# Attention, then two MLPs on one core: later and wider-spaced preparation of the first weight, and two ordering edges on VectorE and ScalarE

## The chip, the cores and the metric

The kernel runs on one core of a Trainium2 chip. The metric is the device time of one execution in microseconds (us); lower is better. Five engines work side by side: PE (TensorE) multiplies, DVE (VectorE), ACT (ScalarE) and POOL (GpSimd) do elementwise work, and SP (SyncE) issues most of the DMAs.

## The reference

Causal attention with a bias that decays by a running sum, four batches of eight heads, 576 positions, 64 numbers per head; then two MLPs on the 2304 x 512 result, the first with the square of a ReLU between its two weights, the second with a leaky ReLU.

```python
scores = scale * np.matmul(q, k.transpose(0, 1, 3, 2))
bias = -(cum[:, :, :, None] - cum[:, :, None, :])          # cum: running sum of max(s, 0)
scores = np.where(causal, -1000000000.0, scores + np.minimum(bias, 0.0))
attn = np.exp(scores - max); attn = attn / (sum + 1e-09)
x = (attn @ v) as (2304, 512)
x = np.maximum(x @ w_in, 0) ** 2 @ w_out                   # first MLP, 512 -> 2048 -> 512
x = leaky(x @ w2_in) @ w2_out                              # second MLP
```

## The kernel before, in words

**Attention (`attention`, L673 to L875).** The 32 (batch, head) problems go in 16 pairs of heads. Each pair has seven steps (`STEPS`), and a step is called a slot: pair x has slots 7x to 7x + 6, 112 in all. In a slot DVE adds the mask to a block of scores and takes its row minimum of the negated scores (`maxima`, L490), ACT takes the exponentials (L514), PE turns the result over (`flip`, L529), ACT or DVE copies it back (L552, L550), PE multiplies by the values (`values`, L571) and computes the scores of the blocks to come (`scores`, L469 and L457). The first reduction of a pair is the L490 row of form 128x128 at the pair's start.

**The first MLP's first layer (`up1`, L635).** Its 2304 columns are cut into five blocks of up to 512; blocks 0, 1 and 2 are computed inside the attention. `fill` (L774) hands out the matmuls of a block as units of three instructions (L663), three times in a slot, from slot 35 (`START[0]`) on. A block has 16 weight chunks (`fc`) of four units each; when a chunk's four units are issued, `close` (L640) takes the ReLU out of the PSUM bank on ACT (L642), which frees one of two banks called h, and squares it. For block 0 the first eight units go to chunks 0 and 1 in turn, so chunk 2 needs the bank of chunk 0.

**The operand of a block (`up1_x`, L623).** Four pieces of the attention's result are read back and split in a high and a low part: ACT copies the high part (L619), DVE subtracts for the low part (L620).

**The first weight (`load_w`, L158).** It arrives as 64-bit words and is turned into single precision in 16 chunks. A chunk is a job of six steps, one per slot: its first step has SP read 512 KB into one of two buffers (L154, tile `wst`); two steps do nothing; the fourth runs two ACT instructions (L114, L115: the words step); the fifth DVE's L117 and L120 and POOL's addition L122, the last to read the buffer; the sixth casts the high part on ACT (L169, chunks 0 to 9) or DVE (L171, chunks 10 to 15) and subtracts the low part on POOL (L172). The slots are set by

```python
CV = 11
...
at_slot(CV + 5 * fc // 2 + (4 if fc > 7 else 0) + gap, step, job)
```

so chunks 0 to 15 begin in slots 11, 13, 16, 18, 21, 23, 26, 28, 35, 37, 40, 42, 45, 47, 50 and 52. Later weights follow in the same buffers from slot 57 (`convert`).

**What sets the order.** A scheduler orders each engine's instructions by a planned timeline. On PE the order is written out from slot 35 on (`in_order`). `after(i)` adds an edge for the order alone: an instruction traced inside comes behind `i` in the queue if both are on the same engine. The jobs of a slot are traced behind the previous slot's last reduction and last exponential (`anchors`, L866):

```python
with after(*anchors, raw["last"]):
    for f, args in later.pop(y, ()):
        f(*args)
```

After the attention come blocks 3 and 4 and the three remaining layers; the change doesn't touch them.

Of the kernel before, what the change touches and what calls it, by code (L numbers as in the profile page):

```python
# [13 lines left out]
ALU = mybir.AluOpType  # L14
# [4 lines left out]
def f32(ap):  # L19
    return ap.bitcast(F32)  # L20
# [3 lines left out]
def attention_then_two_mlps(  # L24
# [24 lines left out]
    nc = tc.nc  # L49
# [8 lines left out]
    NR1 = S - R  # L58
    W = 512
    LAG = 2  # L60
    CV = 11
    SB, HN = 768, 384
    ORDER = (1, 7, 6, 2, 5, 4, 3)
    CHAIN = {1: 0, 6: 0, 5: 0, 3: 0, 7: 1, 4: 1, 2: 2}
# [307 lines left out]
            self.pT, self.sc, self.po = {}, {}, {}  # L372

    pairs = [Pair(b, g, i) for b in range(B) for g in range(H // 4) for i in range(2)]
    raw = {"fetched": None}

    def load_qk(at, x, i=None, which=(0, 1)):

# [95 lines left out]
    def maxima(at, x, kind, e):  # L474

        p = pairs[x]  # L480
        if kind == 3 and x < PLAIN:
            t = f32(p.Y[:, 3 * e])
        elif kind == 4 and x >= PLAIN:
            t = at.tile([P, S], F32, tag="yt", name="t", bufs=2)
        else:
            t = at.tile([P, S], F32, tag="t", name="t", bufs=TB)
        m = at.tile([P, 16], F32, tag="m", name="m", bufs=TB + 1)

        def reduce(sc, msk, a, z, first, m):
            return nc.vector.tensor_tensor_reduce(t[:, a:z], sc, msk, -QK_SCALE, first, ALU.add, ALU.min, m).ins  # L490

        sc = p.sc[kind][e]
        if kind == 0:
            tiles = ((0, P, 0), (P, 3 * P, 1))
            for a, z, c in tiles:
                done = reduce(sc[:, a:z], mask[:, S - z + a:], a, z, 3.0e38, m[:, c:c + 1])
        elif kind == 4:
            tiles = ((0, S, 0),)
            reduce(sc[:, :S // 2], mask[:, :S // 2], 0, S // 2, 3.0e38, m[:, 1:2])
            done = reduce(p.sc[kind][1][:, :S // 2], mask4, S // 2, S, m[:, 1:2], m[:, 0:1])  # L500
        else:
            tiles = ((0, (kind + 1) * P, 0),)
            done = reduce(sc[:, :(kind + 1) * P], mask[:, S - (kind + 1) * P:], 0, (kind + 1) * P, 3.0e38, m[:, 0:1])
        if kind == 0 and e == 0:
            p.sums = at.tile([P, 16], F32, tag="sums", name="sums", bufs=4)
        T = {0: 0, 2: 2, 3: 3, 4: 4}[kind]
        p.t = t
        return t, m, tiles, p.sums, 2 * T + e, done
# [106 lines left out]
                hs = slice(64 * e, 64 * e + 64)  # L615
                nc.vector.tensor_tensor(p.xo[hs, m:], p.xo[hs, m:], p.rb[4][hs, 64 - 64 * e:P - 64 * e], ALU.mult)

    def split(out, x):
        a = nc.scalar.activation(out[0], x, AF.Copy)  # L619
        b = nc.vector.tensor_tensor(out[1], x, f32(out[0]), ALU.subtract)  # L620
        return a.ins, b.ins

    def up1_x(mp, j, c, bufs):  # L623

        n, w = BLOCKS[j]
        xf = mp.tile([P, w], F32, tag="xf", name="xh", bufs=XF)
        nc.sync.dma_start(xf, xscr[c, :, n:n + w])
        yield
        t = mp.tile([P, 2, w], F32R, tag="xs", name="xs", bufs=bufs)
        xs[j, c] = t  # L630
        split([t[:, z] for z in range(2)], xf)

    xs = {}

    def up1(mp, j, tick=None):  # L635

        n, w = BLOCKS[j]
        group = 2 * W // w

        def close(fc, h, gs):  # L640
            g = gs[:, fc % group]
            done = nc.scalar.activation(g, h[:, :w], AF.Relu)  # L642
            if tick is None:
                nc.scalar.activation(g, g, AF.Square)
            else:
                squared = nc.vector.tensor_tensor(g, g, g, ALU.mult)
            if (fc + 1) % group == 0:
                nc.scalar.dma_start(gscr[fc + 1 - group:fc + 1, :, n:n + w].rearrange("f p t -> p f t"), gs)
            if tick is not None:
                tick(done.ins, squared.ins)  # L650

        order = [(fc, c) for fc in range(FC) for c in range(KC)]
        if tick is None:
            order[:2 * KC] = [(fc, c + x) for x in (0, KC // 2) for fc in range(2) for c in range(KC // 2)]
        todo, hs = None, {}
        for fc, c in order:
            if c == 0:
                if fc % group == 0:
                    gs = mp.tile([P, 2 * W], F32, tag="gs", name="gs", bufs=GB1).rearrange("p (f t) -> p f t", f=group)
                hs[fc] = bank("h")  # L660
            h = hs[fc]
            for y, (a, z) in enumerate(PASSES):
                nc.tensor.matmul(h[:, :w], win[fc][:, a, c * P:(c + 1) * P], xs[j, c][:, z, :w],  # L663
                                 start=(c == 0 and y == 0), stop=(c == KC - 1 and y == 2))
            if todo is not None:
                close(*todo)
                todo = None
            if c == KC - 1:
                todo = (fc, h, gs)
            yield  # L670
        close(*todo)

    def attention(at, mg, mx):  # L673
# [5 lines left out]
        def at_slot(y, f, *args):  # L679
            later.setdefault(y, []).append((f, args))  # L680
# [52 lines left out]
        for j in range(B):  # L733
            for c in range(KC):
                job = up1_x(mx, j, c, XS)
# [24 lines left out]
        for fc in range(FC):  # L760
            job = load_w(fc, wpool, stage)
            for gap in range(6):
                at_slot(CV + 5 * fc // 2 + (4 if fc > 7 else 0) + gap, step, job)
        for ch in range(BEFORE):
            job = convert(*divmod(ch, FC), stage, nc.sync, 3)
            for gap in range(6):
                at_slot(end - 5 * BEFORE // 2 - 8 + 5 * ch // 2 + gap, step, job)
        units, block, done = None, -1, 0
# [43 lines left out]
        for y in range(end + 14):  # L812
            x, st = divmod(y, n)
            if y == START[0]:
                fixed_from = len(nc.cur_bb.bb.instructions)
            if y < end:
                args = maxima(at, x, *STEPS[st])
                live[y] = args[0]
                behind = [args[-1], exponentials(*args[:-1])]
            fill(y, 0)  # L820
            tiled = len(nc.cur_bb.bb.instructions)
            for early in (True, False):
                for px in (x - 1, x):
                    if early or not 0 <= px < len(pairs):
                        continue
                    k0 = y - n * px
                    for region in range(2):
                        if k0 == values_at(px, region):
                            pairs[px].po[region] = values(px, region)
                for z in (y - 3, y - LAG, y - 1):  # L830
                    zx, zs = divmod(z, n)
                    kind, e = STEPS[zs]
                    if early != (kind == 0 and zx < ALONE):
                        continue
                    lag = {2: 3, 3: 1}.get(kind, LAG) if zx >= ALONE else LAG
                    if 0 <= z < end and (e or kind == 4) and y - z == lag:
                        flip(at, zx, kind, [live.pop(i) for i in range(z - e, z + 1)])
            if y + 1 < end and STEPS[(y + 1) % n][1] == 0:
                last = len(KINDS) * x + KINDS.index(STEPS[st][0])
                while asked <= last + (2 if last + 2 < AHEAD else 1):  # L840
                    scores(asked // len(KINDS), KINDS[asked % len(KINDS)])
                    asked += 1
            in_order(tiled, (nc.tensor.engine,))
            divided = [i for i in nc.cur_bb.bb.instructions[tiled:] if i.engine == nc.tensor.engine][-1:]
            for px in (x - 1, x):
                if not 0 <= px < len(pairs):
                    continue
                k0 = y - n * px
                for region in range(2):
                    if k0 == values_at(px, region) + (region or px >= ALONE):  # L850
                        gather(at, px, region, pairs[px].po[region])
                portions = ((5, 8, 9, 0, 2), (8, 11, 12, 2, 5)) if px < ALONE else ((9, 12, 12, 0, 5),)
                for inverted, spread_at, scaled, a, b in portions:
                    if k0 == spread_at and spread_at == scaled:
                        spread(px, a, b)
                    if k0 == scaled:
                        scale(px, a, b)
                    if k0 == inverted:
                        inverse(at, px, a, b)
                    if k0 == spread_at < scaled:  # L860
                        spread(px, a, b)
                if k0 == 12:
                    store(px)
            with after(*divided):
                fill(y, 1)
            with after(*anchors, raw["last"]):  # L866
                for f, args in later.pop(y, ()):
                    f(*args)
            if y < end:
                anchors = behind  # L870
            fill(y, 2)
# [307 lines left out]
```

## Time and profile before

| what | value |
|---|---|
| time, median of 3 runs | 932.47 us (927.65 to 934.24) |
| time of the profiled execution | 930.07 us |
| its span in the profile | 928.3 us |
| PE busy | 896.2 us, 97% of the span |
| DVE, ACT, POOL busy | 696.6, 580.8, 181.3 us |
| mean granted clock of PE | 0.993 of full speed |

The span runs from the first to the last instruction; the execution's own time is 1.8 us longer. Busy time is a union of instructions' times; the idle time of an engine matters where the chain that ends last goes through it.

### The profile page before, as it was taken

To read this page: it belongs to the slowest core of one execution; us is meant where nothing else is said; L and a number is where in the kernel's file an instruction comes from. 1 tells how busy PE (TensorE), PEld (TensorE's weight loads), DVE (VectorE), ACT (ScalarE), POOL (GpSimd) and SP (SyncE) were. 2 spreads that over 40 slices of the span, in tenths; PEclk is the share of its full clock that TensorE was granted. 3 is DMA by queue.
4 is the path that set the end of the run, shared out by engine and by line. 5 is a ranking of instruction groups with operands and counts; after the bars stand their busy time and mean duration, and the time that the engine had idled before them with its cause. 6 is when DMAs were issued, how large, how long until landed. Compare 5 with 4: busy or idle time off the path is not lost.

```text
span 928.3 us, 16360 instructions
## 1 busy us (share of the span) xinstructions
PE 896.2 (97%) x5902; PEld 809.6 (87%) x5902; DVE 696.6 (75%) x1265; ACT 580.8 (63%) x1097; POOL 181.3 (20%) x290
## 2 busy tenths in 40 slices
PE   5879999999999999999999999999999999999997
PEld 3646777777777778989999999999999999999997
DVE  5887666877774277688897997787488697886964
ACT  4788878878885454365555555686587754444442
POOL 4357763343430000001112101001110000000000
PEclk9999999999999999999999999999999999999999
DMA  9766858878853477948649326668668575628303
GB/s 166 173 180 171 223 154 227 224 212 231 231 180 105 126 248 270 317 155 258 218 158 355 112 97 219 215 207 322 239 219 299 176 253 151 183 57 210 81 14 55
DMA packets 229569, 178.48 MB, mean 192 GB/s; under 512 B 139600, under 2 KB 206352, under 8 KB 229488
## 3 DMA queue, kind: packets, MB, share of 16 engines
q1 hardware_dynamic: 192568, 105.13, 41.6%
q10 hardware_dynamic: 27048, 38.16, 11.2%
q0 software_dynamic: 9872, 34.15, 10.6%
q8 instruction: 46, 0.75, 0.3%
q14 instruction: 35, 0.29, 0.1%
HBM read 111.25 MB, written 66.13 MB: 191 GB/s over the span
## 4 chain that ended last, share of the span: by engine, by line
PE 57%; issue 9%; DVE 7%; DMA 5%; POOL 1%; ACT 1%; ACTq 0%; POOLq 0%; DVEq 0%
PE q L881 34%; PE h L663 17%; DVE op L988 3%; PE tr L571 2%; PE S L469 2%; PE tr L529 1%; DMA gp<-gscr 1%; DMA gp<-zscr 1%; DVE gp L982 1%; DMA gp<-qscr 1%; PE S L457 1%; DMA zscr<-post 1%; POOL zscr L1050 1%; DVE wt L119 1%; DVE gp L984 1%
## 5 line engine op out<-in xcount | busy, mean ns | idle before, releaser
L881 PE MATMUL q<-op,w 128*128 128x384 f32 x3024 | 528.3, 335 | 4.1 <-DVE op L988 2.9
L881 PEld LDWEIGHTS q<-op,w 128*128 128x128 f32 x3024 | 523.7, 188 | 8.4 <-DVE op L988 5.6
L987 ACT ACTIVATE op<-gp 128x768 fp32r<-128x768 f32 x189 | 158.3, 846 | 152.7 <-PE q L881 128.6
L663 PE MATMUL h<-xs,w 128*128 128x512 f32 (+1 forms) x960 | 211.7, 375 | 2.0 <-ACT gs L642 2.0
L988 DVE TENSOR_TENSOR op<-gp,op 128x768 fp32r<-128x768 f32 x189 | 178.2, 954 | 40.9 <-ACT op L987 39.6
L663 PEld LDWEIGHTS h<-xs,w 128*128 128x128 f32 x960 | 163.7, 189 | 38.8 <-issue 5.7
L514 ACT ACTIVATE t<-t,m 128x256 f32<-128x256 f32 (+4 forms) x134 | 75.9, 567 | 34.3 <-DVE m L490 32.0
L490 DVE CUSTOM_DVE_ANT_0 t<-S,mask 128x128 f32<-128x128 f32 (+4 forms) x119 | 49.4, 459 | 42.5 <-PE S L469 28.6
L642 ACT ACTIVATE gs<-h 128x512 f32<-128x512 f32 (+1 forms) x80 | 43.6, 547 | 48.0 <-PE h L663 47.7
L185 POOL DMA_DIRECT2D wscr<-wt x48 | 26.5, 553 | 234.9 <-DVE wt L120 234.6
L954 DVE TENSOR_TENSOR post<-q,post 128x768 f32<-128x768 f32 (+1 forms) x55 | 51.6, 940 | 15.7 <-PE q L881 15.2
L469 PE MATMUL S<-Y 64*128 64x128 f32 (+3 forms) x324 | 42.5, 366 | 12.8 <-DVE Y L427 7.6
L934 ACT ACTIVATE post<-q 128x768 f32<-128x768 f32 (+1 forms) x56 | 43.8, 781 | 12.5 <-PE q L881 12.4
L571 PE MATMUL tr<-pT,v 128*64 128x320 f32 (+3 forms) x384 | 48.6, 399 | 2.0 <-ACT pT L552 2.0
L114 ACT ACTIVATE wt<-wst 128x512 f32<-128x512 f32 x64 | 42.3, 660 | 11.2 <-DMA wst<-in_moe_w_in_dram 6.6
L120 DVE SCALAR_TENSOR_TENSOR wt<-wst,wt 128x512 uint32<-128x512 uint32 x64 | 46.7, 731 | 1.1
L914 ACT ACTIVATE post<-post 128x768 f32<-128x768 f32 x36 | 30.4, 845 | 25.8 <-DVE post L954 25.7
L571 PEld LDWEIGHTS tr<-pT,v 128*64 128x64 f32 x384 | 25.7, 141 | 23.3 <-issue 6.6
L117 DVE TENSOR_SCALAR wt<-wt 128x512 uint32<-128x512 uint32 x64 | 30.9, 483 | 19.0 <-ACT wt L114 18.8
L115 ACT ACTIVATE wst<-wst 128x512 uint32<-128x512 uint32 x64 | 42.8, 669 | 2.9 <-DMA wst<-in_moe_w_out_dram 1.7
L198 DVE TENSOR_TENSOR w<-wq,w 128x512 fp32r<-128x512 f32 x49 | 33.3, 688 | 14.4 <-ACT w L197 14.3
L550 DVE COPY pT<-tr 128x512 f32<-128x512 f32 (+1 forms) x64 | 33.7, 549 | 11.4 <-PE tr L529 11.4
(119 smaller groups left out, 931.7 us busy)
## 6 DMA issues: line engine op xcount, KB each, us to landing
gscr<-gs ACTq DMA_DIRECT2D x36, 512.0 KB
gp<-gscr SPq DMA_DIRECT2D x48, 384.0 KB
qscr<-post ACTq DMA_DIRECT2D x48, 384.0 KB
gp<-qscr SPq DMA_DIRECT2D x48, 384.0 KB
wscr<-wt POOLq DMA_DIRECT2D x48, 256.0 KB, 4.0
wst<-in_moe_w_in_dram SPq DMA_DIRECT2D x19, 512.0 KB
wst<-in_moe_w_out_dram SPq DMA_DIRECT2D x16, 512.0 KB
wst<-in_moe_w_out_dram POOLq DMA_DIRECT2D x16, 512.0 KB, 5.0
```

The lines of the kernel that those rows point to most:

```text
L120: nc.vector.scalar_tensor_tensor(t, hw, 0xC0000000, t, ALU.bitwise_and, ALU.bitwise_or)
L469: nc.tensor.matmul(p.sc[kind][e][:, a:z], qs[hs, T * P:(T + 1) * P], ks[hs, :z - a], start=(n == 0 and y == 0), stop=(n == len(tiles) - 1 ...
L490: return nc.vector.tensor_tensor_reduce(t[:, a:z], sc, msk, -QK_SCALE, first, ALU.add, ALU.min, m).ins
L514: done = nc.scalar.activation(t[:, a:z], t[:, a:z], AF.Exp, bias=m[:, c:c + 1], scale=-1.0, accum_out=sums[:, s0:s0 + 1])
L571: p.anchor = nc.tensor.matmul(po[64 * e:64 * e + 64, a:n], p.vr[:, c, e], rhs[e], start=(y == 0), stop=(y == len(mm) - 1), skip_group_chec ...
L642: done = nc.scalar.activation(g, h[:, :w], AF.Relu)
L663: nc.tensor.matmul(h[:, :w], win[fc][:, a, c * P:(c + 1) * P], xs[j, c][:, z, :w], start=(c == 0 and y == 0), stop=(c == KC - 1 and y == 2))
L881: i = nc.tensor.matmul(*args, skip_group_check=True, **kw).ins
L934: done = nc.scalar.activation(t[:, xs], acc, AF.Copy)
L954: done = nc.vector.tensor_tensor(t[:, xs], acc, t[:, xs], ALU.add)
L987: a = nc.scalar.activation(t[:, 0], src, AF.Copy)
L988: c = nc.vector.tensor_tensor(t[:, 1], src, f32(t[:, 0]), ALU.subtract)
```

## The change

It has three parts. The 16 chunks of the first weight begin in other slots: 17, 20, 23, 26, 29 and 32 for chunks 0 to 5, and 34, 36, 39, 41, 43, 45, 48, 50, 52 and 54 for chunks 6 to 15. DVE's subtraction of the operand split (L620) is put behind the last reduction traced so far, for blocks 1 and later. And the jobs of a slot are put, on ACT, behind the ReLU of chunk 0 or 1 of block 0, from when that is traced until chunk 2's is.

```diff
-    CV = 11
...
-    raw = {"fetched": None}
+    raw = {"fetched": None, "reduced": None, "closed": None}
...
-    def split(out, x):
+    def split(out, x, behind=None):
         a = nc.scalar.activation(out[0], x, AF.Copy)
-        b = nc.vector.tensor_tensor(out[1], x, f32(out[0]), ALU.subtract)
+        with after(behind):
+            b = nc.vector.tensor_tensor(out[1], x, f32(out[0]), ALU.subtract)
...
-        split([t[:, z] for z in range(2)], xf)
+        split([t[:, z] for z in range(2)], xf, raw["reduced"] if j else None)
...
             done = nc.scalar.activation(g, h[:, :w], AF.Relu)
+            raw["closed"] = done.ins if j == 0 and fc < 2 else None
...
-                at_slot(CV + 5 * fc // 2 + (4 if fc > 7 else 0) + gap, step, job)
+                at_slot((17 + 3 * fc if fc < 6 else 21 + 9 * fc // 4) + gap, step, job)
...
                 args = maxima(at, x, *STEPS[st])
+                raw["reduced"] = args[-1]
...
-            with after(*anchors, raw["last"]):
+            with after(*anchors, raw["last"], raw["closed"]):
```

## Rows read from the trace of the kernel before

**Rows 1.** Page, busy time of each engine over the span.
```profile
PE 896.2 (97%) x5902; PEld 809.6 (87%) x5902; DVE 696.6 (75%) x1265; ACT 580.8 (63%) x1097; POOL 181.3 (20%) x290
```
**Rows 2.** Windows, one per pair (1 to 6): stretch, length, busy, clock, DMA.
```profile
core 0: us, PE busy (x) PEld busy (x) DVE busy (x) ACT busy (x) POOL busy (x), PEclk, DMA share, GB/s
22.35:34.51 12.16, 10.76 (x123) 7.72 (x121) 9.09 (x34) 8.95 (x28) 2.37 (x9) 1.00 0.62 169
34.51:49.22 14.71, 11.93 (x135) 8.05 (x132) 12.28 (x40) 11.40 (x33) 7.97 (x12) 1.00 0.92 186
49.22:63.05 13.83, 10.90 (x113) 7.67 (x113) 11.25 (x40) 11.98 (x34) 8.60 (x12) 1.00 0.53 163
63.05:76.83 13.78, 11.56 (x93) 7.39 (x95) 11.78 (x41) 11.43 (x31) 8.62 (x11) 0.75 0.92 189
76.83:97.60 20.77, 19.02 (x171) 14.48 (x166) 15.83 (x45) 18.58 (x47) 16.02 (x23) 1.00 0.72 197
97.60:118.38 20.78, 20.78 (x172) 16.12 (x171) 13.92 (x41) 17.35 (x43) 14.38 (x17) 1.00 0.77 194
```
**Rows 3.** Timeline of DVE around the first reductions of pairs 3 and 4.
```profile
49.12 0.19 DVE L588 RECIPROCAL sums<-sums 128x5 f32<-128x5 f32 x1 [1.80 <-ACT sums L587]
49.22 0.25 DVE L490 CUSTOM_DVE_ANT_0 t<-S,mask 128x128 f32<-128x128 f32 x1
...
62.44 0.69 DVE L620 TENSOR_TENSOR xs<-xh,xs 128x512 fp32r<-128x512 f32 x1 [2.51 <-ACT xs L619]
63.05 0.28 DVE L490 CUSTOM_DVE_ANT_0 t<-S,mask 128x128 f32<-128x128 f32 x1
```
**Rows 4.** Timeline of ACT ahead of these two reductions.
```profile
45.46 0.67 ACT L114 ACTIVATE wt<-wst 128x512 f32<-128x512 f32 x1 [1.66 <-DMA wst<-in_moe_w_in_dram]
...
59.47 0.63 ACT L169 ACTIVATE w<-wt 128x512 fp32r<-128x512 f32 x1 [1.59 <-POOL wt L122]
...
61.77 0.64 ACT L619 ACTIVATE xs<-xh 128x512 fp32r<-128x512 f32 x1
```
**Rows 5.** Timeline of PE: the same values' matmuls in pairs 3 and 4.
```profile
53.82 2.16 PE L571 MATMUL tr<-pT,v 128*64 128x320 f32 x16
...
68.39 4.11 PE L571 MATMUL tr<-pT,v 128*64 128x320 f32 x16
```
**Rows 6.** Windows just ahead of the clock's fall and while it was down.
```profile
59.00:65.69 6.69, 4.62 (x56) 3.26 (x52) 4.11 (x18) 5.60 (x16) 5.43 (x7) 1.00 0.75 196
65.69:72.51 6.82, 5.88 (x34) 3.36 (x34) 6.55 (x19) 5.87 (x17) 3.03 (x3) 0.50 0.99 170
```
**Rows 7.** Timeline of ACT and PE at the first ReLU of block 0.
```profile
89.91 0.67 ACT L115 ACTIVATE wst<-wst 128x512 uint32<-128x512 uint32 x1
...
90.47 0.62 ACT L169 ACTIVATE w<-wt 128x512 fp32r<-128x512 f32 x1
90.99 0.58 ACT L642 ACTIVATE gs<-h 128x512 f32<-128x512 f32 x1
...
91.62 3.72 PE L663 MATMUL h<-xs,w 128*128 128x512 f32 x15 [1.75 <-ACT gs L642]
```
**Rows 8.** ACT by line and form, 24 to 160 us: count, busy, mean ns, idle before.
```profile
L115 ACT ACTIVATE wst<-wst 128x512 uint32<-128x512 uint32 x18 | 12.0, 669 | 1.1 <-DMA wst<-in_moe_w_in_dram 1.1
L114 ACT ACTIVATE wt<-wst 128x512 f32<-128x512 f32 x18 | 11.9, 663 | 3.1 <-DMA wst<-in_moe_w_in_dram 3.1
...
L169 ACT ACTIVATE w<-wt 128x512 fp32r<-128x512 f32 x10 | 6.3, 625 | 2.4 <-POOL wt L122 2.4
```
**Rows 9.** Waits of SP's queue, 24 to 160 us: total, times, longest.
```profile
SPq L154 <- POOL wt L122: 15.5, 5, 6.0
```
**Rows 10.** Waits of PE, 97 to 300 us: total, times, longest.
```profile
PE S L469 <- DVE m L490: 1.0, 1, 1.0
PE S L457 <- DVE m L490: 0.4, 1, 0.4
```
**Rows 11.** POOL finishes the last chunk; PE's row that first uses it.
```profile
141.46 1.29 POOL L172 TENSOR_TENSOR w<-wt,w 128x512 fp32r<-128x512 f32 x1 [1.94 <-DVE w L171]
...
154.71 3.02 PE L663 MATMUL h<-xs,w 128*128 128x512 f32 x12
```

## The prediction

> **What bounds the kernel now.** I read the page's busy times first: PE is busy for 97% of the span [rows 1], so what can still be won is PE's idle time and whatever makes PE slow. Next I cut the attention into windows, one per pair, at each pair's first reduction [rows 2]. Two regimes show. From pair 6 on PE is busy in all of 20.78 us, and the list of PE's waits from 97 to 300 us holds only 1.0 and 0.4 us [rows 10]: there PE is the bound and other engines' work is hidden. Pairs 1 to 4 have no filler matmuls; no engine is full in them, and a pair takes as long as its chain of scores, reductions, exponentials and turns. Pair 1, in which only one words step of a weight chunk falls and no cast, takes 12.16 us. Pairs 2, 3 and 4, with two words steps each beside their casts, take 14.71, 13.83 and 13.78: 2.55, 1.67 and 1.62 more, 5.84 in sum. Since PE is full nearly everywhere behind them, a microsecond won here should arrive at the end.
>
> Then I looked for what ends the waits at the starts of pairs 3 and 4. DVE works its queue in order. At 49.12 a reciprocal has waited 1.80 us for ACT, with the first reduction of pair 3 right behind it; at 62.44 the subtraction of an operand split has waited 2.51 us for ACT, with that of pair 4 behind it [rows 3]. ACT was late because weight work stood at the head of its own queue: a words step 1.66 us for its DMA, a cast 1.59 us for POOL's addition [rows 4]. So the weight chunks cost pairs 2 to 4 less by their length than by what queues behind them.
>
> Two more losses show. PE's granted clock was 0.50 from 65.69 to 72.51, which is 1.2 GHz in place of 2.4; in the 6.69 us before, PE had been busy for 4.62 [rows 6]. Sixteen value matmuls took 4.11 us there, and 2.16 one pair earlier [rows 5], 1.95 more. And in pair 5 PE stands 1.75 us until ACT has taken the first ReLU of block 0 out of its bank [rows 7].
>
> **The change part by part.** The sum is made against the profiled execution, 930.07 us (span 928.3). That is 2.4 below the median of 932.47 and inside the runs' 927.65 to 934.24.
>
> *Chunks later, ahead of slot 35.* Counting due slots, the words steps of pairs 2, 3 and 4 (slots 14 to 34) fall from eight (14, 16, 19, 21, 24, 26, 29, 31) to five (20, 23, 26, 29, 32): from three to one in pair 2, three to two in pair 3, and two in pair 4 either way. In the trace the words run some slots late, two to a pair. Pair 2 then holds one words step at its very end and no cast, so it is much like pair 1: of its 2.55 I take 2.0 off. Its buffers are empty, so the words step that waited for its DMA isn't there. Pair 3 keeps two chunks and casts, now three slots apart; a buffer is asked for again six slots after its last chunk began, not five, so waits like those of SP for POOL's addition, 15.5 us in five cases [rows 9], should shrink, and with them ACT's at the head of its queue. I take 0.2 off pair 3 and 0.3 off pair 4, whose two splits for block 0 stay where they are and get no edge. Sum -2.5. Bounds: all of the excess, -5.84, and +1.3, which is what a chunk cost in pair 2 (2.55 over two words steps), if the two chunks of pair 3 bunch up worse than now. I stay near the count of chunks, since the pair with none of their casts is the nearest row.
>
> What is late next in these pairs is PE: pair 1 has 10.76 us of PE in 12.16, so less than pair 1's length isn't to be had without moving scores.
>
> *The clock.* I put it at nothing: it falls again somewhere in pairs 2 to 4, or the time that it gives back is lost in a pair's chain. Its price by the matmul row is 1.95 us [rows 5]. The Trainium skill, "TensorE: Matmul & The Clock Gate", section "Part 1: The HAM clock gate", says that the slow state comes back after PE has been idle and that sustained work releases it. By that rule fewer idle stretches in pairs 3 and 4 would leave the clock up, which is a rival below; the trace agrees so far as the fall came behind 2 us of idle PE in 6.69.
>
> *Chunks later, behind slot 35.* Three more chunks are worked on there, 3 x (0.663 + 0.669 + 0.625) = 5.9 us of ACT [rows 8]. By due slots pair 5 gets the words and casts of chunks 5, 6 and 7; in the trace, where the work lags, it now holds three words steps and four casts as well, so pair 5 changes little. Pair 6 has three words steps now and no cast on ACT, and gets four and two: 1.33 + 1.25 = 2.6 us more against an idle 20.78 - 17.35 = 3.4 [rows 2]. It fits, at 96% of ACT. PE waited for ACT once, 1.75 us, in pair 5 with ACT at 89%, and never in pair 6 at 83%; I take a quarter of that wait, +0.4. Bounds 0 and +5.9. DVE and POOL have more room (13.92 and 14.38 of 20.78). SP issues the same 16 reads; behind a read that waits for a buffer stand the loads of q, k and v for pairs ahead. From slot 34 a buffer is asked for after 4.5 slots of 2.97 us, 13.4 us, longer than the five slots of about 2 us ahead of it, so I cost that at nothing.
>
> *The last chunks.* Chunk 15 begins two slots later, 5.9 us. POOL finishes it at 142.75 now, and PE's row with it starts at 154.71 [rows 11]: 12 us to spare, so nothing; if that were used up, the excess over 12 us would be paid once.
>
> *ACT behind the ReLU.* In the last rows before the ReLU, an L115 and an L169 run from 89.91 to 90.99 [rows 7]. Both were traced in slot 40, behind the ReLU of chunk 0; with the edge they come after it, and PE's stall falls by 1.08. Other due work in slots 39 to 41 (the turn of q, casts) waits for the ReLU too: behind it stand exponentials, and DVE's and POOL's halves of those jobs. Bounds: -1.75, and +1.6 if ACT now stands idle for PE as it did for POOL's addition [rows 4]. I take -1.1.
>
> *The split behind the reduction.* For blocks 1 and later it can only shift DVE's order in a stretch where PE lost 1.4 us in all to DVE [rows 10]. What is behind the moved subtraction is the block's matmuls, due slots later. Bounds -1.4 and +1.8 (a wait like that at 49.12, [rows 3], in the wrong place); I take 0, as PE is full in nearly all of this.
>
> Sum: -2.5 - 1.1 + 0.4 + 0 + 0 = -3.2, so 926.9 us, 0.6% below the median shown. Its own range, from half of the two gains to both plus a microsecond of noise, is 923.5 to 930.
>
> **The rivals.**
>
> *A, all of the chain comes back.* The clock stays at 2.4 GHz, the waits of rows 3 vanish, and pairs 2 to 4 come close to pair 1: -5.0 of 5.84, and all of the 1.75 in pair 5. 930.07 - 6.75 = 923.3. For it: the two stalls of rows 3 alone are 4.3 us. Against: pairs 3 and 4 still hold four chunks and two splits.
>
> *B, nothing.* What the early pairs gain is asked back when the same chunks' work and the same PE work come in pairs 5 and 6, and the ReLU waits for something else: 930. For it: not one instruction is removed, and no engine but PE is full. The Trainium skill, "Perfetto Trace Analysis", section "Identifying the Most-Contended Engine", says that kernels generally improve by improving the most-contended engine; that is PE by rows 1, and by that rule alone this change would give nothing. Against: pairs 1 to 4 aren't bound by PE.
>
> *C, slower.* ACT overflows in pairs 5 and 6. Its idle time there is 2.19 + 3.43 = 5.6 us [rows 2], and 5.9 us of chunk work moves behind slot 35. If the lag of the early chunks goes on, all of it lands in these two pairs, every exponential, turn and ReLU comes late by it, and PE, whose order is fixed, waits it out; a clock fall of 1.95 comes on top: -2.5 + 5.9 + 1.95 = +5.4, 935.4. It decides once ACT has over 20.8 us to do in one of the two pairs.
>
> *D, the weights come late:* each lost microsecond beyond the 12 to spare; about 933 if chunks 14 and 15 lag by another five slots.
>
> **How the numbers follow.** Forecast 0.40, A 0.25, B 0.22, C 0.10, D 0.03. The range of 920.0 to 934.0 holds the forecast, B, D and nearly all of A, with the bound of -5.84 and the runs' own spread; C lies outside. A measurement here tells about 1% from no change, 9.3 us: under 923.1 or over 941.8. Only the lower half of A and a tail of the forecast get under (0.13); C in its worst form gets over (0.03); the rest, 0.84, is within 1%.
>
> **What would show it.** The windows per pair: pair 2 near 12.5 us, pairs 3 and 4 at 13 to 13.7, pair 5 at 19.5 to 20 and pair 6 still near 20.8 with PE full. DVE's wait for the reciprocal at the end of pair 2 gone. PE's wait for L642 at 0.7 or less. The clock: down in pairs 3 or 4 for the forecast, up throughout for A. Wrong would be: pair 2 still over 14, or new PE waits for ACT of 2 us and more in pairs 5 to 7.

## The result, and the profile after

The changed kernel takes 937.64 us (median of 16 runs, 934.65 to 947.32) against 932.38 for the kernel before (16 runs). The ratio is 1.0065, 95% interval 1.0047 to 1.0084: slower, by about 5 us. The forecast was 926.9 in a range of 920.0 to 934.0. The profiled execution took 936.66 us, its span is 934.9 against 928.3, so 6.6 us are to be found.

The windows of the profile after, one per pair from pair 2 to pair 7, cut at the first reductions as in [rows 2] (columns as there):

```profile
33.60:47.69 14.09, 10.84 (x116) 7.42 (x114) 10.21 (x37) 8.83 (x28) 1.95 (x7) 0.98 0.89 183
47.69:60.66 12.97, 12.74 (x128) 8.95 (x124) 12.67 (x39) 11.29 (x33) 7.59 (x12) 0.89 0.61 176
60.66:72.83 12.17, 10.60 (x112) 7.25 (x113) 11.38 (x37) 11.59 (x33) 8.02 (x11) 1.00 0.98 184
72.83:100.43 27.60, 22.92 (x166) 16.83 (x166) 15.90 (x47) 19.23 (x47) 17.36 (x23) 0.94 0.57 150
100.43:123.93 23.50, 20.27 (x164) 14.75 (x164) 14.48 (x42) 19.08 (x47) 13.88 (x16) 1.00 0.76 198
123.93:144.19 20.26, 20.26 (x170) 15.70 (x169) 15.07 (x42) 16.81 (x41) 13.75 (x18) 1.00 0.56 174
```

Set beside [rows 2], pairs 2 to 4 take 39.2 us in place of 42.3, a gain of 3.1. Pair 5 takes 27.6 in place of 20.8 and pair 6 23.5 in place of 20.8: 9.5 lost. Pair 7 gives 0.5 back, pairs 8 to 14 differ by 0.1 in sum. The rest of the 6.6 is outside: pair 2 begins 0.9 us earlier (the last section says why), the stretch from pair 15 to the end takes 1.5 us longer. In pair 5 no engine is full; ACT, the engine that I had feared for, is idle for 8.4 of 27.6 us. So it is a wait, and the timeline of ACT names it:

```profile
76.36 0.63 ACT L168 ACTIVATE w<-wt 128x512 fp32r<-128x512 f32 x1
82.63 0.65 ACT L114 ACTIVATE wst<-wst 128x512 uint32<-128x512 uint32 x1 [5.64 <-DMA wst<-in_moe_w_in_dram]
83.19 0.64 ACT L113 ACTIVATE wt<-wst 128x512 f32<-128x512 f32 x1
83.73 0.60 ACT L513 ACTIVATE t<-t,m 128x384 f32<-128x384 f32 x1
...
84.33 1.13 ACT L618 ACTIVATE xs<-xh 128x512 fp32r<-128x512 f32 x2
```

(Line numbers after the change are one lower up to the split and up to two higher behind it; L114 was L115, L618 was L619.) The words step of chunk 5 stands at the head of ACT's queue for 5.64 us until its read has landed. Behind it stand an exponential of the pair and the last two operand splits of block 0, L618. In the kernel before, the same two splits stand ahead of the words step, which waits 0.97 us for its read, and PE takes the twelve matmuls of these splits without a wait:

```profile
82.63 1.14 ACT L619 ACTIVATE xs<-xh 128x512 fp32r<-128x512 f32 x2
84.73 0.67 ACT L114 ACTIVATE wt<-wst 128x512 f32<-128x512 f32 x1 [0.97 <-DMA wst<-in_moe_w_in_dram]
```
```profile
85.46 3.03 PE L663 MATMUL h<-xs,w 128*128 128x512 f32 x12
```

PE's timeline after shows who paid:

```profile
80.65 0.40 PE L468 MATMUL S<-ag 64*128 64x512 f32 x2
85.00 4.66 PE L664 MATMUL h<-xs,w 128*128 128x512 f32 x12 [3.95 <-ACT xs L618]
...
91.77 3.71 PE L664 MATMUL h<-xs,w 128*128 128x512 f32 x15 [0.73 <-ACT gs L642]
...
113.43 0.98 PE L664 MATMUL h<-xs,w 128*128 128x512 f32 x3 [0.91 <-ACT gs L642]
...
119.92 0.98 PE L664 MATMUL h<-xs,w 128*128 128x512 f32 x3 [1.84 <-ACT gs L642]
```

PE stood 3.95 us for the splits. The clock then ran at half speed for 3.4 us of pair 5 (mean 0.94), so that the twelve matmuls behind the wait took 4.66 in place of 3.03. The wait for the first ReLU fell from 1.75 us [rows 7] to 0.73. In pair 6 two more waits for a ReLU stand, 0.91 and 1.84; ahead of the first of them ACT again waited for a read of the weight, and the ReLU was queued behind:

```profile
109.95 0.66 ACT L113 ACTIVATE wt<-wst 128x512 f32<-128x512 f32 x1 [3.28 <-DMA wst<-in_moe_w_in_dram]
...
112.79 0.59 ACT L642 ACTIVATE gs<-h 128x512 f32<-128x512 f32 x1
```

The second, 1.84, is another case: from 109.95 to 119.26, where its ReLU starts, ACT is busy without a gap, with the work that had piled up and two more words steps.

By the windows PE was idle for 7.9 us of pairs 5 and 6, against 1.8 before; the four waits shown are 7.4 of it. The 3.4 us at half speed cost half of their length, 1.7. The last 1.7 of the 9.5 us are not accounted for.

Why did the read of chunk 5 land so late? The timelines of POOL and SP after, and a row of SP's waits from 60 to 100 us (total, times, longest):

```profile
72.58 1.30 POOL L121 TENSOR_TENSOR wt<-wt,wst 128x512 uint32<-128x512 uint32 x1
...
75.01 1.31 POOL L121 TENSOR_TENSOR wt<-wt,wst 128x512 uint32<-128x512 uint32 x1
```
```profile
75.03 0.95 SPq L627 DMA_DIRECT2D xh<-xscr  x2
76.07 0.93 SPq L153 DMA_DIRECT2D wst<-in_moe_w_in_dram  x2
```
```profile
SPq L627 <- DMA xscr<-xo: 1.4, 2, 1.2
```

The buffers were freed at 73.9 and 76.3. The read of chunk 5 didn't go at 73.9: it stood in SP's queue behind the reads of the last two pieces of block 0 (L627), which wait for the attention's result to be stored. So the reads of chunks 5 and 6 went out together at 76.07, and the first was there at 82.6, 6.6 us later.

### The profile page after: what moved, and what is told of

It reads as the page before. It is cut to its first block, busy times and chain, and to the rows that moved or that the text cites. A ratio compares the mean times of both kernels' runs of the same rounds, so it can differ in the third digit from the quotient of the medians.

```text
span 934.9 us, 16356 instructions
## 1 busy us (share of the span) xinstructions
PE 897.9 (96%) x5902; PEld 810.2 (87%) x5902; DVE 699.8 (75%) x1265; ACT 579.5 (62%) x1097; POOL 178.4 (19%) x290
## 4 chain that ended last, share of the span: by engine, by line
PE 60%; issue 9%; DVE 6%; DMA 3%; ACT 2%; POOL 1%; ACTq 0%; POOLq 0%; DVEq 0%; SPq 0%
PE q L883 38%; PE h L664 16%; DVE op L990 2%; PE tr L570 2%; PE S L468 2%; PE tr L528 1%; DMA gp<-zscr 1%; PE S L456 1%; DMA zscr<-post 1%; POOL zscr L1052 1%; DMA wst<-in_moe_w_out_dram 0%; DVE gp L984 0%; DMA xh<-xscr 0%; ACT w L196 0%; PE tr L605 0%
## 5 line engine op out<-in xcount | busy, mean ns | idle before, releaser
L664 PE MATMUL h<-xs,w 128*128 128x512 f32 (+1 forms) x960 | 214.4, 377 | 8.3 <-ACT xs L618 4.5
L489 DVE CUSTOM_DVE_ANT_0 t<-S,mask 128x128 f32<-128x128 f32 (+4 forms) x119 | 49.6, 458 | 33.3 <-PE S L468 19.9
L956 DVE TENSOR_TENSOR post<-q,post 128x768 f32<-128x768 f32 (+1 forms) x55 | 51.6, 940 | 15.9 <-PE q L883 15.5
L113 ACT ACTIVATE wt<-wst 128x512 f32<-128x512 f32 x64 | 42.3, 661 | 17.5 <-DMA wst<-in_moe_w_in_dram 12.1
L936 ACT ACTIVATE post<-q 128x768 f32<-128x768 f32 (+1 forms) x56 | 43.7, 781 | 12.5 <-PE q L883 12.3
L119 DVE SCALAR_TENSOR_TENSOR wt<-wst,wt 128x512 uint32<-128x512 uint32 x64 | 49.5, 774 | 1.3
L114 ACT ACTIVATE wst<-wst 128x512 uint32<-128x512 uint32 x64 | 42.9, 670 | 9.5 <-DMA wst<-in_moe_w_in_dram 7.2
L570 PE MATMUL tr<-pT,v 128*64 128x320 f32 (+3 forms) x384 | 46.3, 385 | 2.0 <-ACT pT L551 2.0
L528 PEld LDWEIGHTS tr<-ident,t 64*128 64x128 f32 x720 | 28.8, 140 | 17.8 <-issue 7.6
```

Source lines behind the costliest of these rows:

```text
L119: nc.vector.scalar_tensor_tensor(t, hw, 0xC0000000, t, ALU.bitwise_and, ALU.bitwise_or)
L570: p.anchor = nc.tensor.matmul(po[64 * e:64 * e + 64, a:n], p.vr[:, c, e], rhs[e], start=(y == 0), stop=(y == len(mm) - 1), skip_group_chec ...
L936: done = nc.scalar.activation(t[:, xs], acc, AF.Copy)
L956: done = nc.vector.tensor_tensor(t[:, xs], acc, t[:, xs], ALU.add)
```

## The experiments

Theory 1: the slots make the loss, through a words step at the head of ACT's queue. Theory 2: one of the two edges does. The first four runs take the change apart.

**The new slots without the edges**

```diff
-        split([t[:, z] for z in range(2)], xf, raw["reduced"] if j else None)
+        split([t[:, z] for z in range(2)], xf)
...
-            raw["closed"] = done.ins if j == 0 and fc < 2 else None
```

> The new slots without the two edges. Theory 1 (the slots are the loss: in pair 5 a words step stands at the head of ACT's queue and waits 5.6 us for the read of chunk 5, with the operand splits and exponentials behind it): pair 5 is again about 27 us against 20.8, ACT again waits over 4 us for the weight's DMA between 70 and 90 us, and the time is 936 to 940, ratio 1.004 to 1.009. Theory 2 (the edge behind the ReLU or the split makes the loss): pair 5 is near 20.8 and the time 927 to 930.

Measured: 936.82 us, ratio 1.0050 (1.0028 to 1.0072). Pair 5 takes 26.9 us. ACT's and PE's timelines show the same picture without either edge:

```profile
84.09 0.65 ACT L114 ACTIVATE wst<-wst 128x512 uint32<-128x512 uint32 x1 [5.26 <-DMA wst<-in_moe_w_in_dram]
```
```profile
86.46 0.50 PE L663 MATMUL h<-xs,w 128*128 128x512 f32 x1 [3.57 <-ACT xs L618]
```

**Both edges, with the slots of before**

```diff
-at_slot((17 + 3 * fc if fc < 6 else 21 + 9 * fc // 4) + gap, step, job)
+at_slot(11 + 5 * fc // 2 + (4 if fc > 7 else 0) + gap, step, job)
```

> Both edges, with the slots of before. Theory 1: no wait of ACT for the weight's DMA beyond that of before, pair 5 at 19.5 to 20.8 us, time 929 to 932.5, ratio 0.997 to 1.000. Theory 2: the loss is here too, 936 to 940.

Measured: 929.84 us, ratio 0.9987 (0.9971 to 1.0004), pair 5 at 20.7 us. PE is busy in all of that pair, at a mean clock of 0.92.

**The edge behind the ReLU alone, slots of before** (the slots as in the run above, and)

```diff
-        split([t[:, z] for z in range(2)], xf, raw["reduced"] if j else None)
+        split([t[:, z] for z in range(2)], xf)
```

> Only the edge behind the ReLU, with the slots of before. Theory 1: PE's wait of 1.75 us for the first ReLU falls to about 0.7 and the time by about 1 us, 930 to 932.5. Theory 2 with this edge to blame: pair 5 grows by several us and the time is over 935.

Measured: 929.02 us, ratio 0.9979 (0.9957 to 1.0001). Pair 5 takes 20.1 us, at a clock of 1.00, and PE's row behind the first ReLU has no wait left, where 1.75 us stood in [rows 7]:

```profile
88.84 0.58 ACT L642 ACTIVATE gs<-h 128x512 f32<-128x512 f32 x1
```
```profile
89.47 3.70 PE L664 MATMUL h<-xs,w 128*128 128x512 f32 x15
```

The stall is gone; the time just fails to tell itself from no change.

**The edge on the split alone, slots of before** (the slots as there, and)

```diff
-            raw["closed"] = done.ins if j == 0 and fc < 2 else None
```

> Only the edge that puts DVE's part of the split behind the last reduction, with the slots of before. Theory 1: nothing before 140 us changes, as block 0 has no such edge; PE's waits between 150 and 300 us change by 1.4 us at most; 931 to 933. Theory 2 with this edge to blame: pairs 9 and 13, where the splits of blocks 1 and 2 fall, grow and the time is over 935.

Measured: 932.45 us, ratio 1.0004 (0.9980 to 1.0027): nothing. With these four Theory 2 is out: the slots are the loss. The next four ask what in the slots it is: a words step at the head of the queue (1a), or the amount of weight work moved behind slot 35 (1b).

**The changed kernel, words step of chunk 5 three slots later**

```diff
-        for _ in range(3):
+        for _ in range(6 if fc == 5 else 3):
             yield
...
-            for gap in range(6):
+            for gap in range(9 if fc == 5 else 6):
```

> The changed kernel, with the words step of chunk 5 alone due three slots later; its read keeps its slot. In the order of ACT the two instructions then stand behind the operand splits of block 0 and one exponential, no longer ahead of them. Theory 1a (the loss in pair 5 is what is queued on ACT behind the words step that waits for its read): PE's wait of 3.95 us for the splits is gone or under 1.5, pair 5 is 22 to 25 us in place of 27.6, the time 932 to 935.5. Theory 1b (what costs is the amount of weight work behind slot 35, not who stands at the head): pair 5 stays at 26 or more and the time at 936 to 939.

Measured: 932.68 us, ratio 0.9998 (0.9978 to 1.0017), so some 5 us under the changed kernel. But pair 5 is still 27.3 us; that half of the expectation missed, and the timelines of ACT, DVE and PE say why:

```profile
78.17 1.33 ACT L618 ACTIVATE xs<-xh 128x512 fp32r<-128x512 f32 x2 [0.54 <-DMA xh<-xscr]
82.56 0.66 ACT L114 ACTIVATE wst<-wst 128x512 uint32<-128x512 uint32 x1 [3.06 <-DMA wst<-in_moe_w_in_dram]
...
84.32 0.66 ACT L113 ACTIVATE wt<-wst 128x512 f32<-128x512 f32 x1 [0.51 <-DMA wst<-in_moe_w_in_dram]
```
```profile
85.01 0.43 DVE L116 TENSOR_SCALAR wt<-wt 128x512 uint32<-128x512 uint32 x1 [4.67 <-ACT wt L113]
...
88.17 0.68 DVE L489 CUSTOM_DVE_ANT_0 t<-S,mask 128x512 f32<-128x512 f32 x1
```
```profile
80.86 3.03 PE L664 MATMUL h<-xs,w 128*128 128x512 f32 x12
...
89.52 1.09 PE L456 MATMUL S<-Y,last 128*128 128x288 f32 x3 [5.29 <-DVE m L489]
```

The splits now run at 78.17, 6.2 us earlier than in the changed kernel, as soon as their input is there (its reads went out at 75.51 here and at 75.03 there). PE's 3.95 us for them are gone, and the same twelve matmuls take 3.03 us. But another wait comes to the front: DVE's half of a words step, queued ahead of the pair's next reductions, stands 4.67 us for ACT, and PE stands 5.29 for the reduction. The L113 that DVE waits for, at 84.32, waits for a read that landed after the one that the L114 at 82.56 waits for; by the order of the reads it is that of chunk 6, whose words step was not moved. In the changed kernel DVE had stood about as long, beside ACT's own stall:

```profile
83.86 0.43 DVE L116 TENSOR_SCALAR wt<-wt 128x512 uint32<-128x512 uint32 x1 [4.88 <-ACT wt L113]
```

With PE's 5.29 us the clock fell, and it stayed at half speed for 6.8 us, twice as long as in the changed kernel (the pair's mean is 0.88); fifteen matmuls took 5.47 us, 3.71 in the changed kernel at full speed:

```profile
91.60 5.47 PE L664 MATMUL h<-xs,w 128*128 128x512 f32 x15
```

Of the 4.2 us between the spans of the two profiles, 2.6 come in pairs 6 and 7 (41.2 us in sum against 43.8) and 1.4 from pair 15 on. So this run shows that the order on ACT decides what PE waits for; that pair 5 comes back with it, it doesn't show.

**No chunk from slot 30 to 35**

```diff
-at_slot((17 + 3 * fc if fc < 6 else 21 + 9 * fc // 4) + gap, step, job)
+at_slot((17 + 3 * fc if fc < 5 else 26 + 2 * fc) + gap, step, job)
```

> Both edges, chunks 0 to 4 in the new slots, chunk 5 from slot 36 and the rest every two slots to slot 56: no chunk begins between slots 29 and 36, as none does between 28 and 35 in the kernel before. Theory 1a: no wait of ACT for the weight's DMA ahead of the splits, pair 5 at 19.5 to 21.5; what pairs 0 to 4 won (about 4 us) arrives, 927 to 930, unless the closer reads make new waits in pairs 6 to 8. Theory 1b: even more weight work lies behind slot 35, so 937 to 942.

Measured: 930.25 us, ratio 0.9987 (0.9960 to 1.0015). Pair 5 takes 18.6 us, 9 under the changed kernel and 2.1 under the kernel before:

```profile
72.48:91.10 18.62, 18.62 (x157) 14.26 (x158) 14.73 (x44) 17.68 (x44) 14.88 (x21) 1.00 0.66 165
```

The 2.1 are not all won. A window ends at DVE's first reduction, and PE's work can fall into the next one: 157 matmuls stand in this one, 171 in that of the kernel before [rows 2]. Over pairs 5 to 7 it is 61.8 us, against 62.4 before and 71.4 in the changed kernel. Pairs 6 and 7 take 21.9 and 21.2, and a new loss stands in pair 8, 25.7 us against 20.8: PE is idle for 3.0 us of it, and the clock's mean is 0.93.

**The gap, with one chunk more ahead of it**

```diff
-at_slot((17 + 3 * fc if fc < 6 else 21 + 9 * fc // 4) + gap, step, job)
+at_slot((14 + 3 * fc if fc < 6 else 36 + 9 * (fc - 6) // 4) + gap, step, job)
```

> Both edges, chunks 0 to 5 every three slots from slot 14, chunk 6 from slot 36 and then every two and a quarter, to 56. Theory 1a: as the run before, one chunk fewer behind slot 36 and reads further apart, so pair 5 at 19.5 to 21 and 926.5 to 930; pairs 2 to 4 give back about 1 us. Theory 1b: 935 to 939.

Measured: 929.34 us, ratio 0.9973 (0.9953 to 0.9992). Pair 5 takes 18.7, pair 8 24.2. The timelines of SP, ACT and PE in pair 8:

```profile
139.20 5.06 SPq L388 DMA_DIRECT2D qr<-in_q_dram  x4
144.36 0.66 SPq L151 DMA_DIRECT2D wst<-in_moe_w_out_dram  x1
```
```profile
149.07 0.68 ACT L114 ACTIVATE wst<-wst 128x512 uint32<-128x512 uint32 x1 [5.18 <-DMA wst<-in_moe_w_out_dram]
```
```profile
151.18 0.32 PE L605 MATMUL tr<-ident,sums 128*128 128x128 f32 x1 [1.23 <-ACT xo L580]
```

The same kind of wait in another place: the first read of the next weight came behind the loads of k and q in SP's queue, and its words step stood at ACT's head for 5.18 us. PE is idle for only 1.2 us of the 24.2; the window holds 182 matmuls, 173 in the kernel before. Over pairs 5 to 8 this kernel takes 84.1 us, the kernel before 83.2.

**The kernel before without its pause of four slots**

```diff
-at_slot(CV + 5 * fc // 2 + (4 if fc > 7 else 0) + gap, step, job)
+at_slot(CV + 5 * fc // 2 + gap, step, job)
```

> The kernel before without its four slots of pause ahead of chunk 8 (chunks 8 to 15 begin in slots 31, 33, 36, 38, 41, 43, 46 and 48); no edges. Theory 1a: now a read and a words step fall where block 0's last two pieces are read and split, PE waits 2 to 5 us for the splits or the first ReLU in pair 5, 933 to 938. Theory 1b: less weight work behind slot 35 than before, so 929 to 932.

Measured: 937.34 us, ratio 1.0056 (1.0035 to 1.0077), with pairs 5 and 6 at 24.7 and 25.1 us. This kernel has less weight work behind slot 35 than the kernel before, and no edge; it loses as much as the change:

```profile
85.21 0.65 ACT L115 ACTIVATE wst<-wst 128x512 uint32<-128x512 uint32 x1 [3.39 <-DMA wst<-in_moe_w_in_dram]
...
86.91 1.14 ACT L619 ACTIVATE xs<-xh 128x512 fp32r<-128x512 f32 x2
```
```profile
87.58 0.49 PE L663 MATMUL h<-xs,w 128*128 128x512 f32 x1 [2.04 <-ACT xs L619]
```

Theory 1b is out: more work behind slot 35 with a pause gained, less without one lost. The last three runs try to keep the gain of pair 5 without the loss of pair 8.

**The early gap, then every two slots**

```diff
-at_slot((17 + 3 * fc if fc < 6 else 21 + 9 * fc // 4) + gap, step, job)
+at_slot((14 + 3 * fc if fc < 6 else 24 + 2 * fc) + gap, step, job)
```

> Both edges, chunks 0 to 5 from slot 14 every three as in the run with the early gap, the rest from slot 36 every two slots, so that the last begins in 54 and not in 56. In that run pair 5 had gained 2 us and pair 8 lost 3.4, where a words step of the next weight waited 5.2 us for a read that SP issued behind the loads of q and k. If it is the bunching of the last chunks with that weight that costs, pair 8 comes back to 21 and the time is 925 to 928; if the wait only depends on where the next weight's read stands among the loads, pair 8 stays at 24 and the time at 929 to 931.

Measured: 928.54 us, ratio 0.9977 (0.9963 to 0.9992). Pair 8 is back at 19.9 us, better than expected; the time lies between the two ranges, as pairs 6 and 7, where reads now follow each other closer, take 21.5 and 21.7, 2 us more in sum than with the wider spacing. Pairs 5 to 8 take 81.8 us.

**The same, and the later weights three slots later**

```diff
-at_slot(end - 5 * BEFORE // 2 - 8 + 5 * ch // 2 + gap, step, job)
+at_slot(end - 5 * BEFORE // 2 - 5 + 5 * ch // 2 + gap, step, job)
```

> As the run before, and all 19 chunks of the later weights three slots later (from slot 60). On the same theory of a wait at the head of ACT's queue, the words step no longer meets a read stuck behind q and k: pair 8 at 20.8 to 21, 924 to 928. Against it: at the end of the attention the later chunks run up to slot 110 and may hold up pair 15 or the blocks behind it by 1 to 2 us.

Measured: 928.57 us, ratio 0.9977 (0.9961 to 0.9994): no gain over the run before, where pair 8 had nothing more to give, and just over the 928 expected.

**The gap from 36, and the later weights three slots later** (the edit of the run with no chunk from slot 30 to 35, and the one above).

> The run whose chunks 5 and on begin from slot 36 every two slots, with the later weights three slots later. There pair 8 was 25.7 us. On the theory it comes down to 21 to 22 and the time to 925 to 928; if its loss came from chunk 15 itself (56) being late for the matmuls, it stays at 24 to 26 and 929 to 931.

Measured: 927.29 us, ratio 0.9954 (0.9935 to 0.9973), the fastest of the study, with pair 8 at 21.2 us in place of 25.7. In its profile the clock stays up through the whole attention. SP's, ACT's and PE's side of pair 5:

```profile
75.76 0.93 SPq L153 DMA_DIRECT2D wst<-in_moe_w_in_dram  x2
```
```profile
77.38 1.38 ACT L618 ACTIVATE xs<-xh 128x512 fp32r<-128x512 f32 x2 [0.25 <-DMA xh<-xscr]
...
83.25 0.67 ACT L113 ACTIVATE wt<-wst 128x512 f32<-128x512 f32 x1
```
```profile
72.40:91.00 18.60, 18.60 (x157) 14.26 (x158) 14.69 (x45) 17.68 (x44) 14.82 (x21) 1.00 0.66 164
```

The two reads go out at 75.76, as they did at 76.07 in the changed kernel. Here the words step comes at 83.25, with its data there and the splits, exponentials and the ReLU ahead of it, and PE is busy in all of the pair. That pair of profiles says it best: the read goes out as late in both and costs pair 5 nothing here; the words step placed ahead of the splits is what costs. No run moved the words steps of chunks 5 and 6 alone, with every other slot of the changed kernel kept.

## Why the prediction was wrong

The sign was wrong because of one term. Both signs of being wrong that I had named came up: pair 2 over 14 us (14.09), and a new PE wait for ACT of over 2 us (3.95). Point by point:

- **Chunks later, ahead of slot 35: right in sum by luck, not by pair.** I took 2.0, 0.2 and 0.3 us off pairs 2, 3 and 4, 2.5 in sum; they fell by 0.6, 0.9 and 1.6, 3.1 in sum. For pair 2 I had argued that with empty buffers no words step would wait for its DMA. The reads of chunks 0 and 1 were issued together, at 39.42, and ACT and PE show the wait, with the copies that PE needed behind it:

```profile
44.40 0.66 ACT L113 ACTIVATE wt<-wst 128x512 f32<-128x512 f32 x1 [2.91 <-DMA wst<-in_moe_w_in_dram]
```
```profile
46.00 0.58 PE L528 MATMUL tr<-ident,t 64*128 64x64 f32 x11 [1.84 <-ACT xo L580]
```

  Pair 4 gave 1.6 in its place. Its clock was 1.00 and no longer 0.75; how much of the 1.6 is the clock's no run separates (with both edges and the slots of before pair 4 took 13.4 us at 1.00, but with a PE wait of 1.6 us for POOL in it). And SP's waits for POOL's addition, which were to shrink from 15.5 us [rows 9], were 19.3 us from 24 to 160.
- **The clock: put at nothing.** It fell at the border of pairs 2 and 3, as the forecast had it, and in pair 3 that cost nothing: PE was busy for 12.74 of 12.97 us, and for 11.49 of 13.00 in the last run, where the clock didn't fall:

```profile
47.20:60.20 13.00, 11.49 (x126) 8.10 (x122) 12.68 (x40) 11.36 (x33) 7.53 (x13) 1.00 0.63 177
```

  It fell again in pair 5, behind the new wait, and there the fall cost 1.7 us.
- **Chunks later, behind slot 35: the step that failed.** I put +0.4, by comparing the sum of ACT's work with its idle time, and costed the reads at nothing since a buffer comes up again after 4.5 long slots. Pairs 5 and 6 lost 9.5 us, beyond my bound of 5.9 too. The sums were right: ACT was busy for 19.2 and 19.1 us there, within the 20.8 that I allowed. Wrong was to ask only for room. I had seen this very kind of wait in [rows 4] and counted it as a cost of the old slots; I didn't ask where the new slots would put it. The pause between slots 28 and 35 stood in the code that I described, and the new slots fill it just where the last two pieces of block 0 are read (slot 33) and split (slot 38). Taking the pause from the kernel before costs the same 5 us; with a pause in the new slots the 5 us are not there.
- **Rival C had the sign and the place, not the mechanism.** A late ReLU, PE waiting it out and a clock fall came as it said. But an overflow of ACT would have shown ACT full, and it was idle for 8.4 us of pair 5 and 4.4 of pair 6; only the 1.84 us of pair 6 came where ACT had no gap. The Trainium skill, "TensorE: Matmul & The Clock Gate", section "Architectural detail: the array is 16× 32×32, not 1× 128×128", says that ACT and DVE take their instructions strictly in order. The traces agree: the splits ran at 84.3 in the changed kernel, behind the words step, though in the run with that step later the same input, read 0.5 us later, was there at 78.2.
- **ACT behind the ReLU: right by the profile.** -1.1 predicted; alone it took the whole wait of 1.75 us away, 0.7 off pair 5 and 0.8 off pair 6. The ratio of 0.9979 (0.9957 to 1.0001) fits that and doesn't rule out nothing. In the changed kernel 0.73 was left, as a cast ahead of the ReLU waited for POOL.
- **The split behind the reduction: right,** at nothing (1.0004).
- **The last chunks: right,** no wait for them appeared behind pair 6.
- **The range beside the sum.** Its lower end, 923.5, doesn't follow from its words: both gains and a microsecond give about 925.5.

What stays open: the 1.5 us that the changed kernel's profile loses from pair 15 on. From 300 us on PE's waits there sum to 5.8 us, against 4.3 before: 1.2 more for ACT's L936, 0.6 new for a split, 0.3 less for DVE. Why these grew no run shows, nor what made the read of chunk 5 take 6.6 us.

## What to carry to other kernels

Ahead of moving work between stages, look up for each moved instruction that waits for a DMA what will stand behind it on its engine, and whether its data can be there by then; an engine's idle time says nothing on that. Where a schedule by hand has a pause, find what runs in it before filling it. And when a wait is cut at one engine, look at the other half of the same job: here DVE had stood 4.88 us beside ACT, and with the splits out of ACT's stall PE waited for DVE instead, 5.29 us in place of 3.95.

## What the runs showed of the hardware that was not expected

The clock's falls don't stand still from one execution to the next. Pair 0, which no edit touches, took 12.0 us in three of the profiles (before, the slots alone, the next weight later behind the early gap) and 10.4 in all the others; in just those three the granted clock was at half speed for 3.4 us between 17 and 23 us. So 1.6 us of difference between two single profiles can come from that alone: pair 2 begins 0.9 us earlier after the change as pair 0 is 1.6 shorter and begins 0.6 later. Shares of the loss are better read from windows than from spans.
